# Starting the matmul operands of a three-stage kernel on multiples of 128 bytes in SBUF

## The chip, the core and the metric

The kernel runs on one core of a Trainium2 chip. The metric is the device time of one execution, in microseconds; three executions of the kernel before gave 1410.11, 1410.63 and 1412.31, median 1410.63. The profile is of one more execution.

## The reference

Three layers follow one another, all in float32, for 1536 tokens (2 batches of 768):

- Attention with 8 heads of 64: each query sees the last 128 keys and the first 4 ("sinks"). `a = softmax(scale * q k^T)`, `x = a v`, 1536 x 512.
- The "solu" layer: `h = x @ w_in` (512 to 1024), `u = h * softmax(h)`, a layer norm of `u` with gain `g_ln`, then `x2 = ln @ w_out` (1024 to 512).
- Eight experts: logits `x2 @ w_gate` are balanced by 8 rounds of row and column normalisation to `P`; then for each expert `out += P[:, e] * (relu(x2 @ w1[e]) @ w2[e])`, with `w1[e]` 512 x 1024 and `w2[e]` 1024 x 512. All experts run for all tokens: this is most of the work.

## The kernel before

**Products.** A float32 operand is held as two float32r halves, hi and lo. A product of two operands is three matmuls into the same PSUM bank, hi by hi, hi by lo, lo by hi. The helper `mm3` (L79) issues them, at L80, L82 and L84; in the profile nearly all heavy matmuls stand under these three lines. In each, one operand is stationary (128 x 128, loaded ahead by a weight load, PEld in the profile) and one is moving (128 partitions by up to 512 columns, read from SBUF while the matmul runs).

**Stages.** From 0 to about 300 us the attention of 12 blocks of 128 tokens is interleaved with the solu layer: `h_unit` (L227, moving `w_in` in the weight slots, 512 columns, stationary `xt`; output `hp`) and `x2_unit` (L294, moving `lt`, the transposed layer norm output, 256 columns, stationary `w_out` in the weight slots; output `x2p`). From about 303 us `experts` (L611) runs: for each expert and each of 3 groups of 512 tokens, 96 matmuls with moving `x2T` and stationary `w1` (output tile `p1`), then 96 with moving `w2` and stationary `ht`, the relu'd hidden layer (output `p2`); 4608 in all, each of 512 columns. In the profile both outputs are `p`: `p<-x2T,w` is the first kind, `p<-w,ht` the second. ACT and DVE split each `p1` into `ht` (L659, L660); DVE adds each `p2` to the result (L690). POOL splits the next weights into hi and lo (L73, L77) as slots come free.

**Weight slots.** `w_slot` (L140) deals out slots in a ring: eight tiles `w0` to `w7` of the pool `wp`, and from the expert stage on a ninth, `we0`, in the place that the attention left. The ring of nine meets eight chunks per expert, so each expert has its chunks in other slots, and one chunk is mostly in `we0`.

**Where tiles lie.** A tile's room in a partition is rounded up to a multiple of 32 bytes, no further. Pools on the left grow up from the constants, pools with `side="right"` grow down from the top. The first constant starts at 16512, a multiple of 128; the constants up to `mhalf` (1 float, 32 bytes of room) and `wg_f` take 5920 bytes, so `w0` starts at 22432, which is 32 past a multiple of 128. Each further tile of the left side inherits this, until the three `st` tiles (L238, 12 floats, 64 bytes of room each) move it by 64. The top of the right side lies 32 bytes under a multiple of 128. This gives, in bytes past a multiple of 128 (slices of a tile start at multiples of 512 bytes within it, so this is also where every operand of the tile starts):

| tiles | use | before | after |
|---|---|---|---|
| `w0`..`w7` | stationary for `x2T` and `lt`, moving for `ht` and `xt` | 32 | 0 |
| `we0` | the same, experts only | 96 | 0 |
| `x2T` | moving | 96 | 0 |
| `ht` | stationary | 96 | 0 |
| `lt` | moving | 96 | 0 |
| `xt` | stationary | 96 | 0 |
| `wg_r` | stationary, 32 or 8 columns | 0 | 0 |

**Order.** The planner orders instructions by priority from their order in the program; a tile of a later pool waits for the tiles whose bytes it takes over. The functions that the diff touches:

Of the kernel before, what the change touches and what calls it, by code (L numbers as in the profile page):

```python
# [8 lines left out]
F32 = mybir.dt.float32  # L9
# [6 lines left out]
P = 128  # L16
# [5 lines left out]
def tile_sink_attention__then__solu_moe__then__sinkhorn_moe(  # L22
# [14 lines left out]
):  # L37
    """float32 operands are held as hi + lo, both float32r and exact together; a
    product is hi*hi + hi*lo + lo*hi, accumulated in float32."""
    nc = tc.nc  # L40
# [45 lines left out]

    # ------------------------------------------------------------------ constants
    const = pool(ctx, "const")
# [35 lines left out]
    def set_flag(tmp):  # L124
        """1 where the general path has to do the work."""
        g = tmp(4)
        nc.gpsimd.tensor_scalar(g[:, 0:1], val[:, 0:1], float(NSINK), None, ALU.is_gt)
        nc.gpsimd.tensor_scalar(g[:, 1:2], val[:, 1:2], 1.0, None, ALU.is_lt)
        nc.gpsimd.tensor_scalar(g[:, 2:3], val[:, 1:2], float(P), None, ALU.is_gt)
        nc.gpsimd.tensor_tensor(g[:, 0:1], g[:, 0:1], g[:, 1:2], ALU.add)  # L130
        nc.gpsimd.tensor_tensor(g[:, 0:1], g[:, 0:1], g[:, 2:3], ALU.add)
        nc.gpsimd.tensor_scalar(flag, g[:, 0:1], 0.5, None, ALU.is_gt)

    # ------------------------------------------------------------------ weights
    wraw = wpool = None
# [17 lines left out]
    def w64_load(tp, src):  # L153
        """float64 values as int32 pairs: low word, high word."""
        raw = tp.tile([P, F // 2, 2], I32, name="raw64", tag="raw64", bufs=4)
        nc.sync.dma_start(out=raw.rearrange("p n t -> p (n t)"), in_=src)
        return raw

    def w64_split(tp, raw, dst):
        """float64 to hi + lo: hi is sign, exponent and the upper 11 bits of the mantissa, lo  # L160
        the rest at that exponent. Under float32's range: zero."""
        lo, hi = raw[:, :, 0], raw[:, :, 1]
        n = F // 2
        m = tp.tile([P, n], I32, name="m64", tag="m64", bufs=2)
        a = tp.tile([P, n], I32, name="a64", tag="a64", bufs=2)
        r = tp.tile([P, n], F32, name="r64", tag="r64", bufs=2)
        nc.vector.tensor_scalar(a, hi, 0x7FFFFE00, None, ALU.bitwise_and)
        nc.scalar.activation(out=a, in_=a, func=ACTF.Relu, scale=8.0, bias=low)
        nc.vector.scalar_tensor_tensor(
            out=a, in0=hi, scalar=-0x80000000, in1=a, op0=ALU.bitwise_and, op1=ALU.bitwise_or  # L170
        )
        nc.vector.tensor_scalar(m, hi, 0x1FF, None, ALU.bitwise_and)
        nc.scalar.activation(out=r, in_=lo.bitcast(U32), func=ACTF.Copy, scale=2.0 ** -52)
        nc.gpsimd.tensor_scalar(m.bitcast(F32), m, 2.0 ** -20, 0.0, ALU.mult, ALU.add)
        nc.gpsimd.tensor_tensor(r, r, m.bitcast(F32), ALU.add)
        nc.scalar.activation(out=dst[:, 0], in_=a.bitcast(F32), func=ACTF.Copy)
        nc.vector.tensor_scalar(m, a, -0x800000, None, ALU.bitwise_and)
        nc.gpsimd.tensor_tensor(dst[:, 1], r, m.bitcast(F32), ALU.mult)
# [25 lines left out]

    # ------------------------------------------------------------------ solu layer
    ln = {}

    class Later:
        """Work put off to a later slot of the schedule."""

# [16 lines left out]
    def h_unit(t, xt, pp, later, tr_q):  # L227
        """h = x @ w_in, solu, and the norm, for one block of 128 tokens."""
        hp = pp["h"].tile([P, F], F32, name="hp", tag="h")
        for kk in range(KD):  # L230
            for half in range(F // 512):
                sl = slice(half * 512, half * 512 + 512)
                for _ in mm3(
# [3 lines left out]
                    yield 0.217  # L237
        st = pp["st"].tile([P, 12], F32, name="st", tag="st", bufs=3)  # L238
        u = pp["u"].tile([P, F], F32, name="u", tag="u", bufs=pp.get("nu", 2))
# [54 lines left out]
    def x2_unit(p, pp):  # L294
        """x2^T = w_out^T @ ln^T for two blocks of 128 tokens."""
        lt = ln.pop(p)
        dst = x2T[p // 2]
        cs = slice((p % 2) * 2 * P, (p % 2 + 1) * 2 * P)
        for d2 in range(KD // 2):
            ps = pp["mm"].tile([P, 2, 2 * P], F32, name="x2p", tag="mm")  # L300
            for dd in range(2):
                for f in range(KF):
                    c0 = (f % 2) * DM + (2 * d2 + dd) * P
                    wt = wout_t[f // 2][:, :, c0:c0 + P]
                    rh, rl = (lt[:, i, f].rearrange("p a b -> p (a b)") for i in range(2))
                    for _ in mm3(ps[:, dd], wt[:, 0], wt[:, 1], rh, rl, f == 0, f == KF - 1):
                        yield 0.109
            ds = slice(2 * d2, 2 * d2 + 2)
            split_psum(dst[:, 0, ds, cs], dst[:, 1, ds, cs], ps)

    # ------------------------------------------------------------------ attention
    def load_head_block(tp, src, b, i, tag, bufs):
# [10 lines left out]
    def make_masks(cp, tmp):  # L323
        """1e9 where a key of the block's columns is masked, 0 where it is kept."""
        dif, col, kd, kp, kc, ka = (tmp(P) for _ in range(6))
# [30 lines left out]
    def sink_mask(cp, tmp):  # L356
        """m[p, h] = 1 where row p (three times all heads' sinks) holds a sink of head h."""
        x_i, x, m, z = (tmp(H)[0:96] for _ in range(4))
# [14 lines left out]
    class Fast:  # L373
        """Blocks of 128 queries against their own keys, the block before, and the sinks."""

# [16 lines left out]
        def split_sinks(self):  # L392
            """The sinks' v, block-diagonal over the heads: rows hi, hi, lo."""
            full = self.ap.tile([P, H, D], F32, name="vs_f", tag="xs", bufs=2)[0:96]
# [10 lines left out]
        def q_tr(self, t):  # L405
            """q^T, scaled."""
            ps = pairs_T(self.raw.pop(("q", t)), self.pp)
            qt = self.ap.tile([P, 2, NP, P], F32R, name="qT", tag="qT", bufs=2)
            self.qT[t] = qt

            def evac():
                split_psum(qt[:, 0], qt[:, 1], ps, mul=-scale)

            return evac

        def k_tr(self, t):
            """k^T, in a ring of three blocks, each with the sinks' keys behind it."""
            ps = pairs_T(self.raw.pop(("k", t)), self.pp)
# [49 lines left out]
        def take_sinks(self, pg):  # L468
            """Two heads' probabilities of the sinks, three times."""
            t, pr = divmod(pg, NP)  # L470
# [8 lines left out]
        def a_tr(self, pg):  # L479
            """Transposes of two heads' probabilities."""  # L480
            t, pr = divmod(pg, NP)
# [13 lines left out]
        def sink_tr(self, t):  # L495
            """The sinks' probabilities, transposed: rows hi, lo, hi."""
            ps = self.pp["tr"].tile([96, P], F32, name="trs", tag="tr")
# [25 lines left out]
        def av_sinks(self):  # L523
            """The sinks' part of all heads."""
            nc.tensor.matmul(
# [4 lines left out]
        def x_norm(self, t):  # L530
            """All heads of x over (sum + 1e-9)."""
            sm = self.sums.pop(t)
# [13 lines left out]

    # ------------------------------------------------------------------ sinkhorn experts
    def logits_units(lp, ps_pool, lg):
        """Logits of all tokens, token-major: lg[:, t, e]."""
        nc.gpsimd.tensor_scalar(wg_r[:, :, 0:E], wg_f, 1.0, 0.0, ALU.mult, ALU.add)  # L550
# [22 lines left out]
    def sinkhorn(lp, ps_pool, pr):  # L573
        """pr[:, t, e] = the balanced gate; a generator that yields where PE should go on."""
        lg = lp.tile([P, T, E], F32, name="lg")
# [121 lines left out]

    # ------------------------------------------------------------------ schedule
    def moe_pools(stack):
# [7 lines left out]
    def fast_path(stack):  # L707
        nonlocal wraw, wpool
        wpool = pool(stack, "wp")
        att, att2, early, psum_a = (ExitStack() for _ in range(4))  # L710
        a2 = pool(att2, "att2")
# [56 lines left out]
        def beside():  # L768
            """Work that the scheduler may interleave with what follows it."""
            return tc.high_priority(offset=0)  # L770
# [98 lines left out]
    def general_path(stack):  # L869
        """Any window and any number of sinks: all keys of a head against a block of queries."""  # L870
        nonlocal wraw, wpool
# [102 lines left out]
    with ExitStack():  # L974
        mhalf = const.tile([P, 1], F32, name="mhalf")
        wg_f = const.tile([P, KD, E], F32, name="wg_f")
# [40 lines left out]
```

## Time and profile before

| | |
|---|---|
| median of three executions | 1410.63 us |
| profiled execution, first to last instruction | 1408.0 us |
| PE (TensorE matmul) busy | 1379.9 us, 98% |
| PEld (weight loads) busy | 1125.6 us, 80% |
| DVE, ACT, POOL busy | 412.5, 296.9, 350.3 us |
| granted TensorE clock, mean | 0.991 |

The span stands 2.6 us under the median of the timed executions. A busy PE counts a matmul from its issue to its modelled end, so matmuls overlap in it: the pace of the matmuls is read from the times at which they start, in the timeline. The 16 DMA engines are busy under a tenth of the time after the first 100 us or so, apart from bursts of weight loads.

### The profile page before, as it was taken

How to read it: one execution, taken by the hardware profiler on the slowest of the kernel's cores; microseconds unless marked ns; L12 is line 12 of the kernel's file. 1: busy time of each engine (PE TensorE's matmuls, PEld its weight loads, DVE VectorE, ACT ScalarE, POOL GpSimd, SP SyncE). 2: the span in 40 equal slices, each digit the busy share in tenths (PEclk: the TensorE clock that was granted, in tenths of full speed). 3: DMA queues.
4: the chain of work that ended last, by engine and by line, in shares of the span. 5: the costliest groups of instructions: out<-in, count | busy, mean ns of one | idle time of the engine just before them, and what ended most of it. 6: DMA issues, size and time to landing. Idle time of an engine off the chain costs nothing.

```text
span 1408.0 us, 15901 instructions
## 1 busy us (share of the span) xinstructions
PE 1379.9 (98%) x6599; PEld 1125.6 (80%) x6599; DVE 412.5 (29%) x860; ACT 296.9 (21%) x628; POOL 350.3 (25%) x360
## 2 busy tenths in 40 slices
PE   7799999999999999999999999999999999999998
PEld 5678888887888888888888888888888888888886
DVE  6975645442223121121111121112111111112211
ACT  5765545431111110011001110011100111011100
POOL 7862111145005400420250034004400440042000
PEclk9889999999999999999999999999999999999999
DMA  7411111013002100210020012002100210020000
GB/s 211 144 37 38 38 38 24 16 46 105 1 0 60 60 1 1 60 60 0 17 74 31 0 41 79 1 1 60 60 0 0 61 60 0 0 61 24 23 30 33
DMA packets 68354, 56.24 MB, mean 40 GB/s; under 512 B 39984, under 2 KB 56368, under 8 KB 68272
## 3 DMA queue, kind: packets, MB, share of 16 engines
q1 hardware_dynamic: 68272, 55.13, 13.5%
q8 instruction: 54, 0.88, 0.3%
q14 instruction: 28, 0.23, 0.1%
HBM read 51.97 MB, written 3.15 MB: 39 GB/s over the span
## 4 chain that ended last, share of the span: by engine, by line
PE 92%; DVE 3%; ACT 1%; issue 0%; POOL 0%; ACTq 0%
PE p L80 25%; PE p L82 25%; PE p L84 25%; PE av L518 2%; PE x2p L80 2%; PE x2p L82 2%; PE x2p L84 2%; PE hp L84 1%; PE hp L80 1%; PE hp L82 1%; PE trp L490 1%; PE sc L80 1%; PE trp L320 1%; PE trp L276 1%; PE sc L82 1%; PE sc L84 0%
## 5 line engine op out<-in xcount | busy, mean ns | idle before, releaser
L659 ACT ACTIVATE ht<-p 128x512 fp32r<-128x512 f32 x192 | 115.0, 599 | 866.8 <-PE p L84 866.8
L80 PE MATMUL p<-x2T,w 128*128 128x512 f32 x672 | 266.5, 397 | 0.0
L82 PE MATMUL p<-x2T,w 128*128 128x512 f32 x672 | 266.0, 396 | 0.0
L84 PE MATMUL p<-x2T,w 128*128 128x512 f32 x672 | 265.3, 395 | 0.0
L80 PE MATMUL p<-w,ht 128*128 128x512 f32 x672 | 262.8, 395 | 0.0
L84 PE MATMUL p<-w,ht 128*128 128x512 f32 x672 | 262.5, 394 | 0.0
L82 PE MATMUL p<-w,ht 128*128 128x512 f32 x672 | 262.5, 394 | 0.0
L660 DVE SCALAR_TENSOR_TENSOR ht<-p,ht 128x512 fp32r<-128x512 f32 x192 | 132.8, 692 | 426.4 <-ACT ht L659 426.4
L73 POOL TENSOR_SCALAR w<-wr 128x1024 fp32r<-128x1024 f32 x56 | 58.7, 1050 | 628.9 <-PE p L84 620.0
L690 DVE SCALAR_TENSOR_TENSOR acc<-p,pr,acc 128x512 f32<-128x512 f32 x84 | 63.1, 751 | 394.9 <-PE p L84 394.9
L84 PEld LDWEIGHTS p<-w,ht 128*128 128x128 f32 x672 | 125.8, 187 | 30.9
L80 PEld LDWEIGHTS p<-x2T,w 128*128 128x128 f32 x672 | 126.7, 189 | 29.5
L84 PEld LDWEIGHTS p<-x2T,w 128*128 128x128 f32 x672 | 126.7, 189 | 29.5
L80 PEld LDWEIGHTS p<-w,ht 128*128 128x128 f32 x672 | 125.9, 187 | 30.5
L82 PEld LDWEIGHTS p<-w,ht 128*128 128x128 f32 x672 | 125.9, 187 | 30.3
L82 PEld LDWEIGHTS p<-x2T,w 128*128 128x128 f32 x672 | 126.8, 189 | 28.5
L77 POOL TENSOR_TENSOR w<-wr,w 128x512 fp32r<-128x512 f32 x112 | 144.0, 1307 | 4.3
L80 PE MATMUL x2p<-lt,w 128*128 128x256 f32 x192 | 55.8, 291 | 0.2
L82 PE MATMUL x2p<-lt,w 128*128 128x256 f32 x192 | 55.4, 289 | 0.0
L84 PE MATMUL x2p<-lt,w 128*128 128x256 f32 x192 | 54.3, 283 | 0.0
L518 PE MATMUL av<-v,at 128*128 128x64 f32 x352 | 52.7, 294 | 0.6 <-ACT at L493 0.5
L518 PEld LDWEIGHTS av<-v,at 128*128 128x128 f32 x352 | 49.8, 214 | 3.6 <-ACT at L493 1.5
(173 smaller groups left out, 1510.4 us busy)
## 6 DMA issues: line engine op xcount, KB each, us to landing
wr<-in_moe_w_dram SPq DMA_DIRECT2D x64, 512.0 KB, 3.4
raw<-in_moe_w_in_dram SPq DMA_DIRECT2D x8, 512.0 KB, 5.6
raw<-in_moe_w_out_dram SPq DMA_DIRECT2D x8, 512.0 KB, 3.7
qk<-in_q_dram SPq DMA_DIRECT2D x12, 256.0 KB, 3.0
qk<-in_k_dram SPq DMA_DIRECT2D x12, 256.0 KB, 2.9
v<-in_v_dram SPq DMA_DIRECT2D x12, 256.0 KB, 3.0
out_dram<-acc SPq DMA_DIRECT2D x12, 256.0 KB, 2.0
gains<-in_moe_g_ln_dram SPq DMA_DIRECT2D x1, 512.0 KB, 5.5
```

The lines of the kernel that those rows point to most:

```text
L73: nc.gpsimd.tensor_scalar(hi, src, 1.0, 0.0, ALU.mult, ALU.add)
L77: nc.gpsimd.tensor_tensor(lo[:, cs], src[:, cs], f32(hi[:, cs]), ALU.subtract)
L80: nc.tensor.matmul(ps, lhsT=lh, rhs=rh, start=start, stop=False)
L82: nc.tensor.matmul(ps, lhsT=lh, rhs=rl, start=False, stop=False)
L84: nc.tensor.matmul(ps, lhsT=ll, rhs=rh, start=False, stop=stop)
L276: nc.tensor.transpose(ps[:, j], u[:, f * P:(f + 1) * P], ident)
L320: nc.tensor.transpose(ps[:, j], src[:, 2 * j:2 * j + 2].rearrange("p h d -> p (h d)"), ident)
L490: nc.tensor.transpose(ps[:, hh, z], a[:, o:o + P], ident)
L518: nc.tensor.matmul(self.av_ps[:, h], lhsT=at[:, hh, z], rhs=self.raw["v", tv][:, h], start=h == 0 and n == 0, stop=h == H - 1 and n == len ...
L659: nc.scalar.activation(out=ht[:, 0], in_=ps, func=ACTF.Relu)
L660: nc.vector.scalar_tensor_tensor(out=ht[:, 1], in0=ps, scalar=0.0, in1=f32(ht[:, 0]), op0=ALU.max, op1=ALU.subtract)
L690: nc.vector.scalar_tensor_tensor(out=acc[t], in0=ps, scalar=pr[:, t, e:e + 1], in1=acc[t], op0=ALU.mult, op1=ALU.add)
```

## The change

Three tiles get more room, and nothing reads or writes the room that is added. No instruction is added or removed.

```diff
-        st = pp["st"].tile([P, 12], F32, name="st", tag="st", bufs=3)
+        st = pp["st"].tile([P, 32], F32, name="st", tag="st", bufs=3)
...
     def fast_path(stack):
         nonlocal wraw, wpool
         wpool = pool(stack, "wp")
+        pool(stack, "edge", side="right").tile([P, 248], F32, name="edge")
...
-        mhalf = const.tile([P, 1], F32, name="mhalf")
+        mhalf = const.tile([P, 25], F32, name="mhalf")[:, 0:1]
```

`mhalf` now takes 128 bytes instead of 32, so the left side starts at 22528, a multiple of 128; each `st` takes 128 instead of 64; `edge` takes 992 bytes at the top of the right side, which brings the tiles under it to multiples of 128. The left side's tiles rise by 96 bytes, and by 288 behind the `st` tiles; the right side's fall by 992. The other lines of the diff take out comments.

## Rows read from the trace of the kernel before

**Rows 1.** Span and mean granted clock; busy time of each engine from the page.

```profile
core 0: 1408.0 us, clock 0.991
...
PE 1379.9 (98%) x6599; PEld 1125.6 (80%) x6599; DVE 412.5 (29%) x860; ACT 296.9 (21%) x628; POOL 350.3 (25%) x360
```

**Rows 2.** The chain that ended last, by engine and by line.

```profile
PE 92%; DVE 3%; ACT 1%; issue 0%; POOL 0%; ACTq 0%
PE p L80 25%; PE p L82 25%; PE p L84 25%; PE av L518 2%; PE x2p L80 2%; PE x2p L82 2%; PE x2p L84 2%; PE hp L84 1%; PE hp L80 1%; PE hp L82 1%; PE trp L490 1%; PE sc L80 1%; PE trp L320 1%; PE trp L276 1%; PE sc L82 1%; PE sc L84 0%
```

**Rows 3.** Busy time by stage; columns PE, PEld, DVE, ACT, POOL, clock, DMA, GB/s.

```profile
20.00:100.00 80.00, 68.37 (x316) 54.28 (x317) 72.04 (x150) 54.84 (x125) 64.56 (x60) 0.87 0.39 113
100.00:200.00 100.00, 99.55 (x711) 85.00 (x710) 57.37 (x168) 54.45 (x143) 16.84 (x26) 1.00 0.16 35
200.00:302.70 102.70, 101.60 (x708) 87.52 (x707) 49.46 (x139) 48.16 (x118) 20.41 (x27) 1.00 0.11 29
302.70:345.80 43.10, 41.65 (x263) 34.58 (x262) 12.48 (x22) 9.27 (x17) 30.46 (x25) 1.00 0.28 86
402.30:1402.00 999.70, 999.58 (x4308) 808.40 (x4306) 193.61 (x291) 110.57 (x184) 204.14 (x173) 1.00 0.10 31
```

**Rows 4.** Waits of 402 to 1402 us: engine, line, releaser, us, times, longest.

```profile
ACT ht L659 <- PE p L84: 831.3, 176, 24.6
POOL w L73 <- PE p L84: 620.0, 29, 84.5
...
DVE acc L690 <- PE p L84: 394.9, 84, 5.2
```

**Rows 5.** Groups of PE matmuls by line and shape: count, busy us, mean ns.

```profile
L80 PE MATMUL p<-x2T,w 128*128 128x512 f32 x672 | 266.5, 397 | 0.0
...
L80 PE MATMUL p<-w,ht 128*128 128x512 f32 x672 | 262.8, 395 | 0.0
...
L80 PE MATMUL x2p<-lt,w 128*128 128x256 f32 x192 | 55.8, 291 | 0.2
...
L82 PE MATMUL hp<-w,xt 128*128 128x512 f32 x96 | 41.4, 432 | 0.0
...
L80 PE MATMUL p<-we,ht 128*128 128x512 f32 x96 | 37.6, 392 | 0.0
...
L80 PE MATMUL p<-x2T,we 128*128 128x512 f32 x96 | 37.4, 389 | 0.0
```

**Rows 6.** Timeline of PE, moving `x2T`, weights in `w6`, `w7`: start us, us.

```profile
600.18 0.40 PE L84 MATMUL p<-x2T,w 128*128 128x512 f32 x1
...
608.58 0.40 PE L84 MATMUL p<-x2T,w 128*128 128x512 f32 x1
```

**Rows 7.** The same, directly after, weights in `we0`.

```profile
611.34 0.39 PE L84 MATMUL p<-x2T,we 128*128 128x512 f32 x1
...
614.74 0.39 PE L84 MATMUL p<-x2T,we 128*128 128x512 f32 x1
```

**Rows 8.** The same, directly after, weights in `w0`.

```profile
616.12 0.39 PE L84 MATMUL p<-x2T,w 128*128 128x512 f32 x1
...
619.55 0.39 PE L84 MATMUL p<-x2T,w 128*128 128x512 f32 x1
```

**Rows 9.** The same, directly after, moving weights, stationary `ht`.

```profile
623.03 0.39 PE L84 MATMUL p<-w,ht 128*128 128x512 f32 x1
...
625.13 0.39 PE L84 MATMUL p<-w,ht 128*128 128x512 f32 x1
```

**Rows 10.** Timeline of PE, `x2_unit`, 256 columns, at two places.

```profile
291.41 0.28 PE L84 MATMUL x2p<-lt,w 128*128 128x256 f32 x1
...
292.77 0.28 PE L84 MATMUL x2p<-lt,w 128*128 128x256 f32 x1
...
307.98 0.28 PE L84 MATMUL x2p<-lt,w 128*128 128x256 f32 x1
...
310.10 0.28 PE L84 MATMUL x2p<-lt,w 128*128 128x256 f32 x1
```

**Rows 11.** The tile `lgp` (gate logits): ns min/median/max, first and last start.

```profile
L561 PEld LDWEIGHTS lgp<-x2T,wg_r x12: 87/88/92, 304.5 to 336.1; 128*8 128x8 f32 x12
L561 PE MATMUL lgp<-x2T,wg_r x12: 390/396/398, 304.7 to 336.4; 128*8 128x512 f32 x12
```

**Rows 12.** Timeline of PE, scores, 264 columns; moving `kl`, `kh` 0 and 64 past 128.

```profile
170.79 0.28 PE L82 MATMUL sc<-kl,qT 64*128 64x264 f32 x1
170.91 0.28 PE L84 MATMUL sc<-kh,qT 64*128 64x264 f32 x1
```

## The prediction

> **What bounds the kernel now.** I read the span and the busy times first, then the chain of waits, the busy time by stage, the waits, and last the timeline of PE. PE is busy 98% of the span [rows 1], and the chain that ended last is PE for 92%, three quarters of it the three lines of the expert matmuls [rows 2]. In the expert stage PE is busy 999.58 of 999.70 us at a granted clock of 1.00, which is the 2.4 GHz level [rows 3]; the other engines wait for it there: ACT 831.3 us for the matmul that ends a product, POOL 620.0 us for slots to come free, DVE 394.9 us [rows 4]. So only the pace of the matmuls counts, and work elsewhere is hidden with hundreds of microseconds to spare.
>
> The pace is what the reader is to look at. At 2.4 GHz one column a cycle would be 512 / 2.4 = 213.3 ns for a matmul. The stage has 4308 matmuls in 999.70 us, 232.1 ns each (a handful of them are tiny) [rows 3]. That is 18.7 ns too many on each, with no idle time, so something within the matmul stream costs 8%. The timeline shows that the excess is not one number:
> - weights in `w6`, `w7`: 36 matmuls from 600.18 to 608.58, 8.40 / 36 = 233.3 ns [rows 6];
> - the next weights, in `we0`, the same `x2T`: 15 from 611.34 to 614.74, 3.40 / 15 = 226.7 ns [rows 7];
> - the next, in `w0`: 15 from 616.12 to 619.55, 3.43 / 15 = 228.7 ns [rows 8];
> - then moving weights with stationary `ht`: 9 from 623.03 to 625.13, 2.10 / 9 = 233.3 ns [rows 9].
>
> The durations of the groups say the same of the whole run: 397 ns with weights in `w`, 389 in `we0`; with `ht` 395 and 392 [rows 5]. What sets `we0` apart is where it starts: `x2T`, `ht` and `we0` all lie 96 bytes past a multiple of 128, `w0` to `w7` lie at 32. The pair with equal starts is the fastest. For 256 columns (`lt` at 96, `w` at 32) there are two paces, 1.36 / 12 = 113.3 ns and 2.12 / 18 = 117.8 ns [rows 10]; the first is exactly half of 226.7. So 226.7 reads as 17 cycles for every 16 columns, in proportion to the columns, and 233.3 as one more step of 6.7 ns (16 cycles) on a matmul of 512.
>
> **The change part by part.** Instructions, their order and their DMAs stay; only addresses move.
>
> *Experts.* After the change moving and stationary operands all start at 0, so every pair has equal starts, as only `x2T` with `we0` has now. I take its 226.7 ns as the pace of all. Main stage: 4308 x 226.7 = 976.5 us for 999.70, a gain of 23.2 us. The other 300 or so of the 4608 expert matmuls run before it, at 5.4 ns each 1.6 us. Together 24.8 us. Bounds: below, nothing gained, or a loss (the rivals); above, one column a cycle, 213.3 ns, 4608 x 18.7 = 86 us. I take 226.7 because it is the nearest row: the same moving tile, shapes and loop, with equal starts.
>
> *Solu layer.* `hp` has 3 x 96 = 288 matmuls of 512 columns, moving `w` at 32, stationary `xt` at 96, the pairing that runs at 233.3 in the experts [rows 5, 9]: 288 x 6.7 = 1.9 us. `x2p` has 576 of 256 columns; at 117.8 going to 113.3 all of them would give 2.6 us, and some are at 113.3 already [rows 10]; I take two thirds, 1.7 us. From 100 to 302.7 us PE is busy 201.15 of 202.70 us [rows 3], so what is saved there shows; from 20 to 100 us PE is busy 68.37 of 80, with DVE busier at 72.04 [rows 3], and a shorter matmul only lengthens a wait. A sixth of the 3.6 us may be lost there: I count 3 us, between 0 and 4.5. As the matmuls shrink, ACT and DVE (about half busy in that stretch) are late next, not before.
>
> *Padding.* The unused room costs no time by itself. But the left side moves up by 96 to 288 bytes and the right side down by 992, so in the stretch where the expert tiles take over the room of the attention a tile may wait for another predecessor. PE stands idle there for 43.10 - 41.65 = 1.45 us [rows 3]; it can lose at most that or gain a like amount, so I take 0, between -1.45 and +1.5. The DVE, ACT and POOL operations get new starts too; behind the waits of rows 4 a change of theirs in either direction is hidden. If POOL became slower by all of its 204 us of that stage [rows 3], its 620 us of waiting would still cover it.
>
> *Sum.* 1408.0 - 24.8 - 3 = 1380.2 us of span; with the 2.6 us by which the median stands above the profiled span, 1382.8; since a pace takes some steps to settle after a pause or another stage I allow 1 us: 1384 us, 1.9% under 1410.6. The likeliest case's own range is 1378 to 1392.
>
> The stationary operand's load is not what takes the time: in the gate logits only 8 columns are loaded, in 88 ns, and the matmul beside it still has 396 ns, the duration that goes with 233 [rows 11]. So the excess belongs to reading the moving operand, and its size to how that read falls.
>
> **The rivals.**
>
> *A. The excess goes wholly.* Both starts that the trace has, 32 and 96, are 32 past a multiple of 64. If a read that starts on a line has no extra cycle at all, the pace is 213.3 ns: 86 us for the experts, 288 x 20 = 5.8 us and 576 x 11 = 6.3 us for the solu layer, about 1313 us; half of the step, 220 ns, would give some 54 us and 3, about 1352 us. For it: every operand of the heavy loops is off such a line, and all are slow. Against: score matmuls of 264 columns with moving operands at 0 and 64 start 0.12 us apart [rows 12], where one column a cycle is 0.110 (they run on half the partitions, two heads beside each other, so this is weak). The Trainium skill's page "TensorE: Matmul & The Clock Gate" (section "Back-to-back issue gap") has N / 2.4 + 2.5 ns for warm matmuls, 215.8 at 512 columns. The trace disagrees by 11 to 17 ns [rows 6, 7], so it does not hold for these operands as they lie; by it the kernel would come to about 1326 us. I give 8 in 100 to the whole, 8 to about half.
>
> *B. No change.* The pace depends on something else that `we0` has, its place high in SBUF near `x2T`, or what went before: `w6` has 233.3 and `w0` 228.7 with the same starts [rows 6, 8], so the start alone does not decide. Then it is 1410.6 us as before, give or take 1.5. The Trainium skill's page "SBUF — State Buffer" (section "Door 1: The DMA port swizzle", the box on cachelines) speaks for it: SBUF has lines of 16 bytes, and multiples of 32 are on such a line already. By that rule the change would do nothing. The trace does not bear it out as the whole story, since paces of 226.7 and 233.3 stand side by side. 14 in 100. A partial gain, where all settle at 228.7 or thereabouts, is 4608 x 3.4 = 16 us, 1395 us: 10 in 100.
>
> *C. Slower.* With every tile at 0 the two read streams of PE, and the writes of `ht` by ACT and DVE, all reach a line's end at once. If that collides, each matmul takes a step more than the slowest now, 240 ns: (240 - 232.1) x 4608 = 36 us, and 2 for the solu layer, 1449 us; a third of it, 1422 us. It decides from a pace above 232.1 ns on. For it: two of the paces differ by exactly one such step, so steps exist and a third is conceivable. Against: `x2T`, `we0` and `ht` all start at 96 and are the fastest of all. 10 in 100.
>
> **How the numbers follow.** The forecast has 50 in 100, the partial gain 10, A 16, B 14, C 10. Three timed runs and the spread of before (0.15%) tell 0.2% from no change, about 3 us. Faster: 50 + 10 + 16 = 76; same 14; slower 10. For 8 in 10 the range runs from 1345, which takes in the half of A and leaves out the whole (8), to 1414, which takes in B and leaves out nearly all of C (10).
>
> **What would show it.** In the timeline of the expert stage all weights, whatever slot, should step at 226.7 ns (34 matmuls in 7.71 us), and the durations of `p<-x2T,w` and `p<-w,ht` should fall from 397 and 395 to 389, as `p<-x2T,we` has now; the stage of 4308 matmuls should take 976 us, with idle time still near zero. `x2p` should step at 113.3 throughout. A pace near 213 to 220 means A; `w` still at 233 while `we0` stays at 226.7 means B; above 233, C. PE idle of more than 3 us between 300 and 346 us would mean that I priced the new waits wrongly. The prediction is wrong if the stage's mean pace is outside 225 to 229 ns.

## The result and the profile after

The changed kernel takes 1385.47 us (four runs, 1384.35 to 1386.08) against 1410.37 for the kernel before (1409.78 to 1412.31): a ratio of 0.9821, 95% interval 0.9807 to 0.9835. The forecast was 1384.

The profiled execution has a span of 1382.6 us, 25.4 less than before [rows 1]. The first fence is the core's span and clock; the second the stages, the main one cut where the last expert matmul has started (columns as in [rows 3]).

```profile
core 0: 1382.6 us, clock 0.992
```

```profile
100.00:200.00 100.00, 99.56 (x714) 85.38 (x713) 57.95 (x170) 54.96 (x145) 17.42 (x26) 1.00 0.15 35
200.00:302.70 102.70, 101.62 (x706) 87.80 (x705) 49.36 (x136) 47.61 (x116) 19.80 (x27) 1.00 0.11 29
302.70:345.80 43.10, 41.66 (x262) 34.59 (x261) 12.05 (x22) 9.26 (x17) 30.29 (x25) 1.00 0.28 86
...
402.30:1376.00 973.70, 973.70 (x4300) 806.62 (x4300) 192.43 (x286) 110.21 (x184) 202.58 (x173) 1.00 0.10 32
```

4300 matmuls in 973.70 us are 226.4 ns each (a handful are tiny) where 4308 took 999.70. PE is as busy as before, its clock is the same 1.00, and between 302.7 and 345.8 us it idles for the same 1.44 us as before (1.45): the padding made no new wait. The matmuls themselves follow each other faster. The others still wait for PE:

```profile
ACT ht L659 <- PE p L84: 809.1, 176, 23.9
POOL w L73 <- PE p L84: 601.9, 29, 81.9
```

The groups of PE, to be held against [rows 5] (count, busy us, mean ns):

```profile
L80 PE MATMUL p<-x2T,w 128*128 128x512 f32 x672 | 262.0, 390 | 0.0
...
L80 PE MATMUL p<-w,ht 128*128 128x512 f32 x672 | 259.4, 390 | 0.0
...
L80 PE MATMUL x2p<-lt,w 128*128 128x256 f32 x192 | 56.1, 292 | 0.2
...
L82 PE MATMUL hp<-w,xt 128*128 128x512 f32 x96 | 41.3, 430 | 0.0
...
L80 PE MATMUL p<-x2T,we 128*128 128x512 f32 x96 | 37.4, 389 | 0.0
```

The four kinds of expert matmul, which had 397, 395, 392 and 389 ns, now have one duration. The timeline has one pace for all of them: from `we0` on into `w0`, and in the products with `ht` (start us, us).

```profile
605.04 0.39 PE L84 MATMUL p<-x2T,we 128*128 128x512 f32 x1
...
609.12 0.39 PE L84 MATMUL p<-x2T,we 128*128 128x512 f32 x1
...
611.84 0.39 PE L84 MATMUL p<-x2T,w 128*128 128x512 f32 x1
...
622.04 0.39 PE L84 MATMUL p<-w,ht 128*128 128x512 f32 x1
...
624.76 0.39 PE L84 MATMUL p<-w,ht 128*128 128x512 f32 x1
```

18 steps in 4.08 us, 12 in 2.72 us and 12 in 2.72 us: 226.7 ns each, where before the three stood at 226.7, 228.7 and 233.3 [rows 7 to 9].

Only `x2p` went the other way. Before, its matmuls of 256 columns had two paces, 113.3 and 117.8 ns [rows 10]. Now, at about the same place:

```profile
307.62 0.28 PE L84 MATMUL x2p<-lt,w 128*128 128x256 f32 x1
...
310.14 0.28 PE L84 MATMUL x2p<-lt,w 128*128 128x256 f32 x1
```

21 steps in 2.52 us, 120.0 ns.

### The profile page after: what moved, and what is told of

It reads as the page before. It is cut to its first block, busy times and chain, and to the rows that moved or that the text cites. A ratio compares the mean times of both kernels' runs of the same rounds, so it can differ in the third digit from the quotient of the medians.

```text
span 1382.6 us, 15901 instructions
## 1 busy us (share of the span) xinstructions
PE 1354.8 (98%) x6599; PEld 1125.9 (81%) x6599; DVE 411.9 (30%) x860; ACT 296.6 (21%) x628; POOL 348.1 (25%) x360
## 4 chain that ended last, share of the span: by engine, by line
PE 92%; DVE 3%; ACT 1%; issue 0%; POOL 0%
PE p L80 25%; PE p L84 25%; PE p L82 25%; PE av L518 2%; PE x2p L80 2%; PE x2p L82 2%; PE x2p L84 2%; PE hp L84 1%; PE hp L80 1%; PE hp L82 1%; PE trp L490 1%; PE trp L320 1%; PE sc L80 1%; PE trp L276 1%; PE sc L82 1%; PE sc L84 0%
## 5 line engine op out<-in xcount | busy, mean ns | idle before, releaser
L80 PE MATMUL p<-x2T,w 128*128 128x512 f32 x672 | 262.0, 390 | 0.0
L82 PE MATMUL p<-x2T,w 128*128 128x512 f32 x672 | 261.5, 389 | 0.0
L84 PE MATMUL p<-x2T,w 128*128 128x512 f32 x672 | 261.5, 389 | 0.0
L80 PE MATMUL p<-w,ht 128*128 128x512 f32 x672 | 259.4, 390 | 0.0
L82 PE MATMUL p<-w,ht 128*128 128x512 f32 x672 | 258.9, 389 | 0.0
L84 PE MATMUL p<-w,ht 128*128 128x512 f32 x672 | 258.9, 389 | 0.0
```

What stands on the lines that cost most here:

```text
L80: nc.tensor.matmul(ps, lhsT=lh, rhs=rh, start=start, stop=False)
L82: nc.tensor.matmul(ps, lhsT=lh, rhs=rl, start=False, stop=False)
L84: nc.tensor.matmul(ps, lhsT=ll, rhs=rh, start=False, stop=stop)
```

## The experiments

The first theory, E, is the prediction's: equal starts modulo 128 give 226.7 ns, wherever they are. Its rivals were Z (each operand has to start on a multiple of 128, as the change's words have it) and R (place or history). After the first four runs a third came up, M: what counts is the distance between the two starts, modulo more than 128. "Distance" below is the start of the stationary operand less the start of the moving one, in bytes. For the tiles of the kernel it is worked out from their sizes and order; a trace holds no addresses.

### Two maps of starts, all operands at 96, and the left side alone

The maps are small kernels of nothing but chains; the matmul of a chain is the line

```
nc.tensor.matmul(ps[0:c, 0:n], lhsT=stt[:, so:so + c], rhs=mvt[:, mo:mo + n], start=(i == 0), stop=(i == count - 1))
```

with `so` and `mo` at chosen starts. Paces of the maps are mean times from start to start over the second half of a chain. (In the first two maps the stationary tile lies 128 past a multiple of 256 from the moving one; that mattered.)

> A kernel that holds only chains of 48 matmuls (128 x 128 stationary, 512 columns moving, float32r), one chain for each pair of starts 0, 16, 32 .. 112 bytes past a multiple of 128 (8 x 8 pairs), all pairs twice in two orders; it computes nothing of the reference. Theory E (equal starts): a pair with equal starts settles at 226.7 ns from start to start, wherever it starts; unequal pairs settle at 229 to 233. Rival Z (zero): only starts at 0 are fast, the pair 0, 0 at 226.7, the pairs 32, 32 and 96, 96 at 233, and a pair with one start at 0 lies between. Rival R (place or history): the pace does not follow the starts; the same pair has different paces in its two orders.

> Only chains again, nothing of the reference: starts 0, 32, 64, 96 for both operands, each pair twice, in three forms: 256 columns moving; 512 columns with only 8 stationary columns; bfloat16 operands of 512 columns. Theory E: at 256 columns equal pairs 113.3 ns, others 115 to 118; at 8 stationary columns the load is short, so the pace is the same for every pair if the two reads are what collide (226.7), and follows the moving start alone if it is not; bfloat16 reads half the bytes, so no pair shows the excess (213.3 to 216 ns). Rival Z: all three forms follow the moving start, 0 the fastest.

```diff
-        pool(stack, "edge", side="right").tile([P, 248], F32, name="edge")
...
-        mhalf = const.tile([P, 25], F32, name="mhalf")[:, 0:1]
+        mhalf = const.tile([P, 17], F32, name="mhalf")[:, 0:1]
```

> The changed kernel with every operand of the heavy loops 96 bytes past a multiple of 128 (mhalf 17 floats, no edge; st as in the change). Theory E: all pairs have equal starts, 226.7 ns throughout, 1384 to 1387 us, a ratio of 0.982 to before. Rival Z (a multiple of 128 is what counts): nothing starts on a multiple of 128, so 1410 us, ratio 1.00.

```diff
-        pool(stack, "edge", side="right").tile([P, 248], F32, name="edge")
```

> The change without the edge tile: weights w0 to w7, lt and xt at 0; x2T, ht and we0 stay at 96. Theory E: in the experts only the pairs with we0 are equal; the others stay at 229 to 233 ns, 1400 to 1411 us; hp and x2p (now 0 with 0) are as in the changed kernel. Rival Z: each operand at 0 helps by itself; half of the operands of the experts are at 0, so about half of the gain, 1397 us, with the products that move the weights gaining most.

With all operands at 96 the kernel takes 1386.69 us (1386.3 to 1387.7), ratio 0.983 (0.9813 to 0.9846): nearly the whole gain, and no operand of the heavy loops on a multiple of 128. That ends Z. With the left side alone it takes 1413.68, ratio 1.002 (1.001 to 1.0029): no part of the gain, a trace of a loss, though half of the operands of the experts are on multiples of 128. Theory E had 1400 to 1411 us there, so it had the direction and missed the size by 2.7 us; the distances of that kernel are 32 and 224, which the later map has at 233.3 ns. Groups of the first and of the second (count, busy us, mean ns):

```profile
L80 PE MATMUL p<-x2T,w 128*128 128x512 f32 x672 | 262.0, 390 | 0.0
```

```profile
L80 PE MATMUL p<-x2T,w 128*128 128x512 f32 x672 | 266.3, 396 | 0.0
...
L80 PE MATMUL p<-w,ht 128*128 128x512 f32 x672 | 263.6, 396 | 0.0
```

Theory E came through these two but for that size, and fell by the map that should have drawn it. There, in the first of the two orders, the pair 0, 0 has 232.3 ns and the pairs 32, 32, 64, 64 and 96, 96 have 233.3, where theory E has 226.7 for all of them; in the tile view (ns min/median/max, first and last start) the chain of 64, 64 is 48 matmuls in which 10.9 us for 47 steps give 232:

```profile
L41 PE MATMUL xee<-mv,st x48: 392/396/398, 432.4 to 443.3; 128*128 128x512 f32 x48
```

For starts that are multiples of 32 the map goes by the distance, the same along each diagonal: 234.2 to 234.5 wherever the distance is 96, 228.9 at 192, 233.3 at 64 and 160. Only at 128 it has values from 232.1 to 233.3, some of them other in the second order. So R falls as the whole explanation, and a part of it is left: at some distances what ran before counts too (more of this under rival B below). (Starts at odd multiples of 16 give further values, 226.7 among them, some of them different in the two orders; I did not follow these up, as no tile starts there.)

In the second map 8 stationary columns give 231.7 ns at every pair, but for one chain of 231.1. So the pace is that slow with hardly any load (no chain without a load was run); with a full load of 128 columns beside it, it lies above or below, by the distance. At bfloat16 every pair has 215.8 ns. That is what the Trainium skill's page "TensorE: Matmul & The Clock Gate" (section "Back-to-back issue gap") gives for a warm matmul by itself, N / 2.4 + 2.5. For float32r no run here comes down to it. The map at 256 columns gave 113.3 to 120 ns, again by the distance, with 118.5 to 118.8 at equal starts of that map; of the four pairs at distances 64 and 192 three have 113.3 in one order and 117.8 in the other.

### The distance, and four placements in the kernel

> Only chains, nothing of the reference. 512 columns, the moving operand at a multiple of 2048 bytes, one stationary slice 0, 32 .. 2016 bytes behind it; then both 96 further on, four stationary slices 512 bytes apart as in the experts, distance 0 to 480; then that at 256 columns. Theory M (the distance between the two starts counts, modulo 512): 226.7 ns (113.3 at 256 columns) at a distance of 0 modulo 512 in all three forms, also at 96, and at 128, 256 and 384 slower, 229 to 234, as the pair 0, 0 of the first map, whose tiles lay 384 apart modulo 512 and which had 232.3 ns. Theory E (equal modulo 128): 226.7 at every multiple of 128. Rival R: no order in the distance.

```diff
-        pool(stack, "edge", side="right").tile([P, 248], F32, name="edge")
+        pool(stack, "edge", side="right").tile([P, 24], F32, name="edge")
```

> The changed kernel with 96 bytes of edge in place of 992: every operand still starts on a multiple of 128 (the change as its words have it), but x2T, ht and we0 lie 384 past a multiple of 512 while the weights w0 to w7 lie on one. Theory E (equal modulo 128) and rival Z (multiples of 128): 1385.5 us as the changed kernel. Theory M (modulo 512): the gain of the experts goes, pace 232 to 234 ns, 1408 to 1415 us; only the pairs with we0 keep 226.7.

The same line with 120 floats:

> The changed kernel with 480 bytes of edge: x2T, ht, we0 and the weights all on multiples of 512, but no longer of 1024 on the right side. Theory M: 1385.5 us, as the changed kernel. If the distance counts modulo 1024 or more: not all gained; with slices 512 bytes apart half of the products, 1398 us.

With 120 floats, and besides

```diff
+            ap.tile([P, 96], F32, name="gap")
             self.kh = ap.tile([P, NP, 3, C], F32R, name="kh")
...
+        a2.tile([P, 32], F32, name="gap2")
         ap = pool(att, "att")
```

> As the 480-byte edge, and with two unused tiles (128 bytes before the u tiles, 384 before the attention's) that bring lt and xt to multiples of 512 as well. Theory M: x2p falls from 119 ns a matmul in the changed kernel to 113.3, 576 x 5.6 = 3.2 us, of which most shows: 1382 to 1384 us. Theory E: lt and the weights are on multiples of 128 already, 1385.5 us.

The map, ns from start to start by the distance in bytes:

| columns | 0 | 32 | 64 | 96 | 128 | 160 | 192 | 224 |
|---|---|---|---|---|---|---|---|---|
| 512 (8 repeats, 0 to 2016) | 226.7 | 233.3 | 233.3 | 234.3 | 232.2 | 233.4 | 228.9 | 233.3 |
| 512, both 96 further (2 repeats) | 226.7 | 233.3 | 233.3 | 234.4 | 232.6 | 233.4 | 228.9 | 233.3 |
| 256, both 96 further (2 repeats) | 120.0 | 118.3 | 117.8 | 117.3 | 118.6 | 120.0 | 117.8 | 116.7 |

Every 256 bytes the row begins anew, to a tenth of a ns. So the distance counts modulo 256, not 128 and not 512 (as theory M first had it), and the absolute start not at all. In the order of this map a chain at one distance always follows one at the same other distance, so it can't show what history does. Three chains of the map, at distances 0, 256 and 32 (14.3, 14.3 and 14.7 us for 63 steps, the first few unsettled):

```profile
L42 PE MATMUL daa<-mv,st x64: 388/389/398, 37.5 to 51.8; 128*128 128x512 f32 x64
```

```profile
L42 PE MATMUL dba<-mv,st x64: 389/389/397, 631.3 to 645.6; 128*128 128x512 f32 x64
```

```profile
L42 PE MATMUL dab<-mv,st x64: 392/396/397, 824.2 to 838.9; 128*128 128x512 f32 x64
```

The kernels follow it. With 96 bytes of edge all operands are on multiples of 128, exactly as the change is described, and the whole gain is gone: 1411.69 us, ratio 1.0007 (0.9998 to 1.0017), since `x2T` and `ht` now lie 128 from the weights modulo 256. Its groups:

```profile
L80 PE MATMUL p<-x2T,w 128*128 128x512 f32 x672 | 265.9, 396 | 0.0
...
L80 PE MATMUL p<-w,ht 128*128 128x512 f32 x672 | 263.0, 395 | 0.0
```

With 480 bytes (distance 0 again, the starts of the right side no longer on multiples of 1024) it is back: 1385.44, ratio 0.9821 (0.9806 to 0.9836). The kernel that also brings `lt` to distance 0 gained nothing, 1385.82 (0.9811 to 0.9837): at 256 columns distance 0 is among the worst, as the third row of the table has it (120.0), and not the best, as I expected.

### The size of the operands, and `lt` where it was

> Only chains, nothing of the reference; the stationary operand 0, 32 .. 224 bytes behind the moving one, modulo 256 as the second map showed; 128, 192 .. 512 columns moving, then 512 columns with 8, 32, 64 and 96 stationary columns. Theory M (the distance modulo 256, by way of the weight load of the next matmul that reads beside the moving operand): at 512 columns 226.7 ns at distance 0; with fewer stationary columns the distance matters less, with 8 not at all (231.7); each length of the moving operand has its own best distance, as 256 columns have theirs at 224 (116.7) and not at 0 (120). Rival: distance 0 is best at every length but 256.

With the 480-byte edge:

```diff
-        st = pp["st"].tile([P, 32], F32, name="st", tag="st", bufs=3)
+        st = pp["st"].tile([P, 12], F32, name="st", tag="st", bufs=3)
...
+            ap.tile([P, 48], F32, name="gap")
             self.kh = ap.tile([P, NP, 3, C], F32R, name="kh")
```

> As the 480-byte edge, but with st at its 64 bytes again and 192 unused bytes before the attention's tiles: lt comes to the distance from the weights that it had before the change (the weights 64 behind it, modulo 256), xt stays at distance 0. Theory M: the experts as in the changed kernel, x2p back from about 118.6 to 117.8 or 113.3 ns, 576 x 0.8 to 5.3 = 0.5 to 3 us: 1382.5 to 1385 us. Theory E (equal modulo 128): lt is no longer equal to the weights, so x2p becomes slower, 1386 to 1388 us.

| columns moving | 0 | 32 | 64 | 96 | 128 | 160 | 192 | 224 |
|---|---|---|---|---|---|---|---|---|
| 128 and 192 | 111.7 | 111.7 | 111.7 | 111.7 | 111.7 | 111.7 | 111.7 | 111.7 |
| 256 | 120.0 | 118.3 | 113.3 | 117.4 | 118.6 | 119.9 | 113.3 | 116.7 |
| 320 | 146.7 | 146.7 | 146.6 | 146.7 | 146.7 | 146.7 | 146.7 | 146.7 |
| 384 | 173.3 | 173.3 | 176.7 | 173.3 | 176.2 | 176.7 | 173.3 | 176.7 |
| 448 | 206.7 | 204.4 | 202.1 | 206.7 | 204.0 | 205.4 | 200.0 | 200.0 |
| 512 | 226.7 | 233.3 | 233.3 | 234.3 | 232.6 | 233.4 | 228.9 | 233.3 |
| 512, 8 stationary | 231.2 | 231.7 | 231.7 | 231.7 | 231.7 | 231.7 | 231.7 | 231.7 |
| 512, 32 stationary | 231.7 | 230.0 | 231.7 | 230.5 | 230.3 | 233.4 | 231.0 | 233.3 |
| 512, 64 stationary | 229.7 | 231.4 | 232.8 | 226.7 | 229.3 | 231.5 | 228.3 | 230.8 |
| 512, 96 stationary | 230.0 | 228.9 | 228.3 | 233.2 | 231.7 | 231.0 | 233.3 | 226.7 |

The best distance changes with the length and with the width of the load, as theory M has it, and the rival with distance 0 best at every other length falls at 448. One expectation failed: the distance does not matter less with fewer stationary columns until there are hardly any (226.7 to 233.3 ns with 96, 226.7 to 232.8 with 64, 230.0 to 233.4 with 32, 231.2 to 231.7 with 8). Up to 192 columns and at 320 the distance does nothing. At 256 columns and distances 64 and 192 there are two settled paces, 113.3 here and 117.8 in the map before, as in [rows 10], where `lt` lies at distance 64. Distance 0 at 256 columns, in the rows of this map:

```profile
L42 PE MATMUL nca<-mv,st x64: 278/283/302, 151.8 to 159.4; 128*128 128x256 f32 x64
```

and distance 64 (7.1 us for 63 steps where that one has 7.6):

```profile
L42 PE MATMUL ncc<-mv,st x64: 276/276/285, 196.9 to 204.0; 128*128 128x256 f32 x64
```

With `lt` back at distance 64 the kernel takes 1383.85 us, ratio 0.9809 (0.9795 to 0.9822). Whether that is under the changed kernel was tried with both on one chip:

> The changed kernel once more, on the chip of the next run: 1385.5 us.

> The kernel with lt at its old distance once more, on the same chip: theory M 1.5 to 2 us under the changed kernel (x2p at 113.4 to 118 ns for 119); if the difference was between chips, the same as the changed kernel.

The changed kernel has 1385.85 (1384.99 to 1386.57), this one 1383.98 (1383.14 to 1384.35), five runs each and no overlap: 1.9 us faster, the fastest of all tried. Its group shows where:

```profile
L80 PE MATMUL x2p<-lt,w 128*128 128x256 f32 x192 | 55.5, 289 | 0.2
```

289 ns for 292 in the changed kernel and 291 before.

## Why the prediction was right, and where it was not

*Experts, 24.8 us.* Right in size, and in mechanism as far as the pair of starts decides (see "Equal starts"). The pace went to the 226.7 ns of `we0` throughout, as the forecast had it, and the stage's mean of 226.4 lies within its 225 to 229. By the tile view of `p`, from the first matmul with weights in `w` to the last product (before, then after):

```profile
L80 PE MATMUL p<-x2T,w x672: 388/397/502, 333.4 to 1378.7; 128*128 128x512 f32 x168
...
L84 PE MATMUL p<-w,ht x672: 392/394/398, 352.5 to 1400.1; 128*128 128x512 f32 x168
```

```profile
L80 PE MATMUL p<-x2T,w x672: 388/389/500, 333.2 to 1353.9; 128*128 128x512 f32 x168
...
L84 PE MATMUL p<-w,ht x672: 387/389/396, 352.2 to 1374.8; 128*128 128x512 f32 x168
```

1066.7 us became 1041.6, 25.1 less, nearly all of the 25.4 of the span. Taking the price of an unseen placement from the one pairing in the trace that already had it was the step that carried the forecast.

*Solu layer, 3 us.* Mis-sized: 333.4 became 333.2, so it gave 0.2 us. The term of `hp` was right in its pace, 233.3 to 226.7 ns (distance 64 to 0), here over 12 steps at about the same place, 2.80 us before and 2.72 after:

```profile
295.88 0.40 PE L84 MATMUL hp<-w,xt 128*128 128x512 f32 x1
...
298.68 0.40 PE L84 MATMUL hp<-w,xt 128*128 128x512 f32 x1
```

```profile
296.25 0.39 PE L84 MATMUL hp<-w,xt 128*128 128x512 f32 x1
...
298.97 0.39 PE L84 MATMUL hp<-w,xt 128*128 128x512 f32 x1
```

But `x2p`, which I expected at 113.3 ns throughout, went to 118 to 120 and took a part of that back; how much of the rest the waits of the first 100 us hid was not measured. The step that failed here is "the first is exactly half of 226.7": I took the arithmetic of 512 columns over to 256, where `lt` had been at one of the better distances, 64, and the padding of `st` took it to 128.

*Equal starts.* The reason was too wide. I wrote that every pair has equal starts after the change, and the starts were counted modulo 128. That alone would not have done it, as the 96-byte edge shows, which satisfies it and gains nothing. What the change got right is distance 0 modulo 256: 992 bytes of edge, with the 96 of the constants, bring both sides there. For the prediction that was luck, since nothing in the prediction tells 992 bytes from 96. `we0`, `x2T` and `ht` had distance 0 modulo 256 before, so the full-width pairs in the trace of before could not tell 128 from 256. One row spoke against the prediction's "the pair with equal starts is the fastest": `we0` with `ht` has equal starts too, and 392 ns [rows 5]. In the kernel before, it comes six matmuls at a time between products at 233.3 ns, and six are too few to settle (1.38 us, 230.0 ns each):

```profile
1204.17 0.39 PE L80 MATMUL p<-we,ht 128*128 128x512 f32 x1
...
1205.55 0.39 PE L80 MATMUL p<-w,ht 128*128 128x512 f32 x1
```

*The stationary load is not what takes the time.* Half right. The excess is there with a load of 8 columns (231.7 ns), as the row of the gate logits suggested [rows 11]. But with a load of 128 columns the pace lies 5.0 ns below that to 2.6 above it (226.7 to 234.3), by where the load reads, and what the change won lies in this span. The Trainium skill's page "TensorE: Matmul & The Clock Gate" (section "Step-by-step: what each phase is for") has two independent read ports, so that a load takes nothing from the running matmul. For float32r the runs disagree: with the moving operand left where it is, the pace goes from 226.7 to 234.3 ns as the load reads from other places.

*Rivals.* A (no excess at all) is excluded for float32r: no pace in any map at 512 columns is under 226.7. In its lesser case the half of the step is worth (232.1 - 220) x 4608 = 56 us, not 54; its 1352 us go with 56. C (all at 0 collide) did not come at 512 columns; `x2p` at distance 0 is a small case of it. The padding cost nothing, as priced.

B's evidence, `w0` at 228.7 and `w6` at 233.3 with the same starts, is history, and history is real. The pair lies at distance 192, and in the kernel before it has two paces that hold. The last expert shows both with the same weights: behind products with `w` at 233.3 ns the pair keeps 233.3 for all of its 96 matmuls, behind six products with `we0` it has 228.9 for all of them.

```profile
1268.17 0.40 PE L84 MATMUL p<-w,ht 128*128 128x512 f32 x1
1268.41 0.40 PE L80 MATMUL p<-x2T,w 128*128 128x512 f32 x1
...
1290.58 0.39 PE L84 MATMUL p<-x2T,w 128*128 128x512 f32 x1
```

```profile
1312.89 0.39 PE L84 MATMUL p<-we,ht 128*128 128x512 f32 x1
1313.11 0.39 PE L80 MATMUL p<-x2T,w 128*128 128x512 f32 x1
...
1334.86 0.39 PE L84 MATMUL p<-x2T,w 128*128 128x512 f32 x1
```

95 steps take 22.17 us and 21.75 us. In the maps every chain at 192 settled at 228.9, behind slower chains too, so what picks the pace there stays open. History can't stand for the gain: the kernels with edges of 96 and 480 bytes have the same instructions, and the gain goes and comes with the distance. B's other half, that starts on multiples of 32 are alike because all lie on lines of 16 bytes, does not hold here, as placements 32 bytes apart differ.

What stays open is why: where the period of 256 bytes comes from, why the best distance moves with the lengths, and why two paces can hold at one distance. No run here shows it.

## What to carry to other kernels

Where PE is always busy at full clock, compare the time from start to start with columns over clock, group by group; groups that differ with equal shapes differ by something else, here by where their tiles lie. For float32r products of 512 columns with 128 stationary ones place moving and stationary tiles so that their starts differ by a multiple of 256 bytes, and check the pace in the timeline; for other sizes measure the distance first, as none of the eight is best for all. A multiple of 128 for each tile is neither needed nor enough.

## What the runs showed of the hardware that was not expected

- The pace of float32r matmuls depends on the distance of the two operands' starts modulo 256 bytes, and not on either start (512 columns, distances in steps of 32: 226.7 to 234.3 ns; repeated eight times over 2048 bytes).
- float32r never reached a column a cycle at a mean granted clock of 0.996 to 0.997: 226.7 ns at best for 512 columns, 113.3 for 256, where bfloat16 has 215.8 for 512 at every start.
- In chains with 128 stationary columns a float32r matmul took 111.7 ns with 128 columns moving as with 192.
- One distance can have two paces that hold, by what ran before: 113.3 and 117.8 ns at 256 columns (distances 64 and 192), 228.9 and 233.3 ns at 512 (distance 192, in the kernel before).
